# The first softmax of a packed attention: transposes on VectorE in 32x32 blocks, its product with v on tiles of 64 rows

## The chip, the cores and the metric

One core of a Trainium2 chip runs the kernel. The metric is the device time of one execution in microseconds. The kernel before took 729.4 us (median of three runs, 728.02 to 729.69). The engines are PE (matmuls; its weight loads are listed as PEld), DVE (VectorE), ACT (ScalarE), POOL (GpSimd) and SP, which issues most DMAs.

## The reference

The reference is an attention in two steps, followed by a feed-forward network. `q`, `k` and `v` have 8 batches, 8 heads, 576 tokens and 64 columns; `p` has 32 packed rows per head. Everything is float32.

```python
def sm_attn(qq, kk, vv):
    s = scale * np.matmul(qq, kk.transpose(0, 1, 3, 2))
    s = s - np.max(s, axis=-1, keepdims=True)
    a = np.exp(s)
    a = a / (np.sum(a, axis=-1, keepdims=True) + 1e-09)
    return np.matmul(a, vv)
p_packed = sm_attn(p, k, v)           # first softmax: 32 rows over 576 tokens
out = sm_attn(q, p_packed, p_packed)  # second softmax: 576 rows over 32
# x: the heads side by side, 4608 tokens x 512
h = x @ w_in                          # 512 x 2048
g = np.maximum(h, 0.0) + alpha * np.minimum(h, 0.0)
return g @ w_out                      # 2048 x 512
```

`w_in` and `w_out` arrive as 64-bit floats, seen as pairs of 32-bit words, and are converted on the chip.

## The kernel before, in words

**Dense part.** The outer loop runs over 16 halves of a batch (`k`, 288 tokens each) and 16 blocks of 128 hidden columns (`f`). One pair (k, f) is a *turn*. `first` makes the hidden block in PSUM from the second softmax and the product of the packed rows with `w_in` (six matmuls of 128x288 in two-part float32, L577 to L579), and applies the slope on ACT and DVE (L586, L587, L597, L598). `second` multiplies the block of two turns earlier (`AHEAD = 2`) with `w_out` (12 matmuls, L616 to L618). The first sweeps over batch 0 work in plain float32 (L574, L610). Results are evicted (L630 to L636) and stored by SP (L640).

**Attention of a batch** is a generator, `attention(b)`, that yields between its steps: loads; scores of the first softmax (`scores`, L320, through `in_turn`, L310); exponentials; transposes in two bursts; the product with v; the transpose of the packed rows (L449); the scores of the second softmax; then the second softmax itself (L462 to L500).

*First softmax (L354 to L402).* A group `r` (the even or the odd heads) has its four heads' 32 rows on the 128 partitions and all 576 tokens in its columns. ACT copies the scores out of PSUM (L368), DVE takes the maximum of each row (L392), ACT takes the exponential with its sum (L394), DVE makes the reciprocal of the sum (L397, L398). In batch 0 the maxima and exponentials read PSUM (L364, L384).

*Transposes (L409 to L424).* PE turns five blocks of 128 tokens per group against the identity (L419), ten a batch, and ACT evicts them as 384 and 256 columns (L422). The last block overlaps the fourth one by 64 tokens, where v is zeroed by POOL (L285, L296).

*Product with v (L428 to L447).* For each group, each of the five blocks and each of the four pairs of heads a matmul of 128 rows x 32 columns with 64 columns of v (L436), 40 a batch. Four of them lie side by side in the columns of PE's array. ACT scales the result with the reciprocal (L443).

**Loads.** `load` (L166) issues on SP in program order. `load_x` (L258) loads q and k, four tiles of 128 rows per batch; `load_v` (L277) loads v in eight DMAs per batch with runs of 512 bytes (in batch 0: four DMAs with runs of 2048 bytes). `w_in_load` (L218) loads `w_in` in eight pieces of 1 MB, one DMA of 128 rows each.

**Order.** Batches 0 and 1 (`b < EARLY`) are woven into the start and the first turns by hand, in the string given to `go` (L682) and in `pieces` (L699). From batch 2 on, step n of batch b is placed at turn `32 * (b - 1) + 3 + n`, two turns later for n > 7 (L702); a batch has 32 turns. A planner orders the instructions of each engine; `tc.issue_after` fixes what must stand behind what. `in_turn` puts a matmul behind the last dense one; from turn `STRICT = 48` on the dense matmuls keep the written order. In `go`, weight conversions stand behind the last ACT and DVE instructions of the attention's steps so far (`tail`, set by `anchor`, L332).

Of the kernel before, what the change touches and what calls it, by code (L numbers as in the profile page):

```python
# [27 lines left out]
def pack_attention_ffn_kernel(  # L28
# [21 lines left out]
    KT = (S + P - 1) // P  # L50
# [9 lines left out]
    VT = 4  # L60

    const = ctx.enter_context(tc.tile_pool(name="const", bufs=1))
    xin = ctx.enter_context(tc.tile_pool(name="xin", bufs=4))
    vin = ctx.enter_context(tc.tile_pool(name="vin", bufs=4))
# [153 lines left out]
    def w_in_load(n):  # L218
        j, h = n // 2, n % 2
        m = (4, 5, 6, 4, 4, 5, 6, 7)[n]  # L220
        if j == 0:
            src = w_in[:, h * 256 : (h + 1) * 256]
        else:
            src = w_in[2 * h * P : 2 * (h + 1) * P, j * 512 : (j + 1) * 512]
# [33 lines left out]
    def load_x(src, b, pool=None, tags=None, second=None):  # L258

        xs = []
        for pr in range(NP):
            if pool is None:
                x = xin.tile([P, S], F32, name="xraw", tag="xraw")
            else:
                if pr % 2 == 0:
                    two = pool.tile([P, 2, S], F32, name="xtwo", tag=tags[pr // 2])
                x = two[:, pr % 2]  # L270
            load(x, src[b, pr])
            if second is not None and pr == 0:
                load(*second)
            xs.append(x)
        return xs

    def load_v(b, tags=None):  # L277
        vs = []
        for pr in range(NP):
            if tags is None:  # L280
                raw = vin.tile([P, KT, P], F32, name="vraw", tag="vraw")
            else:
                if pr % 2 == 0:
                    two = const.tile([P, 2, KT, P], F32, name="vtwo", tag=tags[pr // 2])
                    nc.gpsimd.memset(two[: KT * P - S, :, VT, :], 0.0)  # L285
                    load(
                        two[:, :, :VT, :],
                        v[b, pr : pr + 2, : VT * P].rearrange("h (kp kt) d -> kp h kt d", kt=VT),
                    )
                    load(  # L290
                        two[KT * P - S :, :, VT, :],
                        v[b, pr : pr + 2, VT * P :].rearrange("h kp d -> kp h d"),
                    )
                vs.append(two[:, pr % 2])
                continue
            nc.gpsimd.memset(raw[: KT * P - S, KT - 1, :], 0.0)  # L296
            load(
                raw[:, : KT - 1, :],
                v[b, pr, : (KT - 1) * P].rearrange("(kt kp) d -> kp kt d", kp=P),
            )  # L300
            load(raw[KT * P - S :, KT - 1, :], v[b, pr, (KT - 1) * P :])
            vs.append(raw)
        return vs
# [6 lines left out]
    def in_turn(b, out, lhs, rhs):  # L310

        with ExitStack() as held:
            if b >= EARLY:
                held.enter_context(tc.issue_after(last_pe[0].ins))
            mm = nc.tensor.matmul(out, lhs, rhs, start=True, stop=True)  # L315
        last_mm[:] = [mm]
        if b >= EARLY:
            last_pe[:] = [mm]
# [12 lines left out]

    def anchor(b, a=None, d=None):  # L332
# [7 lines left out]
    def attention(b):  # L340
        praw = sm.tile([P, NP * N], F32, name="praw", tag="praw", bufs=2)
        packed = praw, pT[b].rearrange("p t n -> p (t n)")
        if b == 0:
            ks = load_x(kT, b, const, ("wo0", "wo1"), packed)
        else:
            load(*packed)
            ks = load_x(kT, b)
        yield
        if b < EARLY:
            vs = load_v(b, ("wo2", "wo3") if b == 0 else None)  # L350
            yield
            qs = load_x(qT, b, *((at, ("a", "a")) if b == 0 else ()))
            yield
        a = d = None  # L354
        in_psum = b < 1
        src, mx = {}, {}
        s_t = [wk.tile([P, S], F32, name="s_t", tag="w") for _ in range(2)]
        for hf in range(2):
            for r, ps in enumerate(scores(b, praw, ks, hf)):
                to = s_t[r][:, hf * HS : hf * HS + HS]  # L360
                if in_psum:
                    src[r, hf] = ps
                    mx[r, hf] = sm.tile([P, 1], F32, name="mx", tag="mx")
                    d = nc.vector.tensor_reduce(out=mx[r, hf], in_=ps, axis=AX.X, op=ALU.max)  # L364
                elif hf == 0 and b == 0:
                    d = nc.vector.tensor_copy(out=to, in_=ps)
                else:
                    a = nc.scalar.copy(out=to, in_=ps)  # L368
# [4 lines left out]
        dens = []  # L373
        for r in range(2):
            nmx = sm.tile([P, 1], F32, name="nmx", tag="nmx")
            den = sm.tile([P, 1], F32, name="den", tag="den")
            if in_psum:
                d = nc.vector.tensor_scalar(
                    out=nmx, in0=mx[r, 0], scalar1=mx[r, 1], scalar2=-SCALE, op0=ALU.max, op1=ALU.mult
                )  # L380
                anchor(b, None, d)
                dh = [sm.tile([P, 1], F32, name="dh", tag="dh") for _ in range(2)]
                for hf in range(2):
                    a = nc.scalar.activation(  # L384
                        out=s_t[r][:, hf * HS : hf * HS + HS], in_=src[r, hf], func=AF.Exp,
                        bias=nmx, scale=SCALE, accum_out=dh[hf],
                    )
                nc.vector.tensor_scalar(
                    out=den, in0=dh[0], scalar1=dh[1], scalar2=EPS, op0=ALU.add, op1=ALU.add
                )  # L390
            else:
                nc.vector.tensor_reduce(out=nmx, in_=s_t[r], axis=AX.X, op=ALU.max, negate=True)  # L392
                nc.vector.tensor_scalar(out=nmx, in0=nmx, scalar1=SCALE, scalar2=None, op0=ALU.mult)
                a = nc.scalar.activation(  # L394
                    out=s_t[r], in_=s_t[r], func=AF.Exp, bias=nmx, scale=SCALE, accum_out=den
                )
                nc.vector.tensor_scalar(out=den, in0=den, scalar1=EPS, scalar2=None, op0=ALU.add)  # L397
            d = nc.vector.reciprocal(out=den, in_=den)  # L398
            dens.append(den)
            anchor(b, a, None if in_psum else d)  # L400
# [3 lines left out]
        if b == 0:  # L404
            aT = [at.tile([P, KT, P], F32, name="aT", tag="a") for _ in range(2)]
        else:
            both = vin.tile([P, KT, 2, P], F32, name="aT", tag="aT", bufs=1)
            aT = [both[:, :, r] for r in range(2)]
        for r in range(2):  # L409
            for t0 in range(0, KT, 3):  # L410
                n = min(3, KT - t0)
                ps = bank()
                for i in range(n):
                    if b == 0 and t0 + i < VT:
# [362 lines left out]
```

## Time and profile before

| | |
|---|---|
| median of three runs | 729.4 us |
| profiled execution | 729.56 us |
| its span on the core | 727.7 us |
| PE busy | 709.6 us |
| DVE, ACT, POOL busy | 427.1, 362.6, 61.1 us |
| read from and written to memory | 70.79 and 13.63 MB |

The profile is of one execution on the chip. Busy time says how long an engine had something in work; matmuls are pipelined, so a busy PE need not be at its peak. The chain of waits is followed back from the last instruction to what released each step. In the rows further down, a line such as L419 is a line of the kernel before; `x5` is a count of instructions, and a float32 matmul has two records where it is made of two passes.

### The profile page before, as it was taken

To read this page: it belongs to the slowest core of one execution; us is meant where nothing else is said; L and a number is where in the kernel's file an instruction comes from. 1 tells how busy PE (TensorE), PEld (TensorE's weight loads), DVE (VectorE), ACT (ScalarE), POOL (GpSimd) and SP (SyncE) were. 2 spreads that over 40 slices of the span, in tenths; PEclk is the share of its full clock that TensorE was granted. 3 is DMA by queue.
4 is the path that set the end of the run, shared out by engine and by line. 5 is a ranking of instruction groups with operands and counts; after the bars stand their busy time and mean duration, and the time that the engine had idled before them with its cause. 6 is when DMAs were issued, how large, how long until landed. Compare 5 with 4: busy or idle time off the path is not lost.

```text
span 727.7 us, 15632 instructions
## 1 busy us (share of the span) xinstructions
PE 709.6 (98%) x6346; PEld 652.7 (90%) x6346; DVE 427.1 (59%) x859; ACT 362.6 (50%) x813; POOL 61.1 (8%) x80
## 2 busy tenths in 40 slices
PE   5799999999999999999999999999999999999998
PEld 3566898898998999999998999989999999999998
DVE  3898988858545474544645465454754538454443
ACT  3686688944435354453544534344444535443332
POOL 1001200002100040000300022000300004000000
PEclk9899999999999999999999999999999999999999
DMA  9996554234136223234034241261331501210001
GB/s 293 387 341 207 205 197 152 69 98 157 56 97 214 68 99 117 80 138 132 34 117 149 70 141 33 107 211 56 112 114 39 179 2 34 87 35 1 33 2 34
DMA packets 51386, 85.44 MB, mean 117 GB/s; under 512 B 4465, under 2 KB 31089, under 8 KB 51313
## 3 DMA queue, kind: packets, MB, share of 16 engines
q1 hardware_dynamic: 51024, 84.14, 34.3%
q8 instruction: 50, 0.82, 0.5%
q10 hardware_dynamic: 288, 0.30, 0.1%
q14 instruction: 24, 0.19, 0.1%
HBM read 70.79 MB, written 13.63 MB: 116 GB/s over the span
## 4 chain that ended last, share of the span: by engine, by line
PE 88%; DVE 5%; ACT 4%; DMA 1%; issue 1%; SPq 1%; ACTq 0%; DVEq 0%
PE acc L616 18%; PE acc L618 17%; PE acc L617 17%; PE ps_h L577 8%; PE ps_h L579 8%; PE ps_h L578 8%; PE ps_m L315 3%; PE ps_j L315 3%; PE ps_m L436 1%; DMA vtwo<-in_v 1%; PE ps_h L574 1%; PE ps_m L419 1%; ACT rest L161 1%; SPq L171 1%; ACT wo L208 1%
## 5 line engine op out<-in xcount | busy, mean ns | idle before, releaser
L616 PE MATMUL acc<-gh,wo 128*128 128x288 f32 x992 | 292.6, 301 | 0.9 <-DVE ot L630 0.7
L617 PE MATMUL acc<-gh,wo 128*128 128x288 f32 x992 | 287.3, 295 | 0.0
L618 PE MATMUL acc<-gl,wo 128*128 128x288 f32 x992 | 266.1, 296 | 0.0
L587 DVE SCALAR_TENSOR_TENSOR neg<-neg,nal,ps_h 128x288 f32<-128x288 f32 x248 | 126.7, 512 | 174.9 <-ACT neg L586 173.8
L616 PEld LDWEIGHTS acc<-gh,wo 128*128 128x128 f32 x992 | 186.1, 188 | 22.0 <-ACT pw L540 10.1
L586 ACT ACTIVATE neg<-ps_h 128x288 f32<-128x288 f32 x256 | 105.1, 411 | 190.1 <-PE ps_h L579 180.3
L617 PEld LDWEIGHTS acc<-gh,wo 128*128 128x128 f32 x992 | 186.3, 188 | 1.2 <-issue 0.8
L618 PEld LDWEIGHTS acc<-gl,wo 128*128 128x128 f32 x992 | 177.3, 188 | 0.1
L598 DVE TENSOR_TENSOR gl<-neg,gh 128x288 fp32r<-128x288 f32 x248 | 120.0, 487 | 68.2 <-ACT gh L597 65.0
L597 ACT CAST gh<-neg 128x288 fp32r<-128x288 f32 x248 | 106.9, 432 | 105.7 <-DVE neg L587 102.3
L579 PE MATMUL ps_h<-a_h,pw 128*128 128x288 f32 x480 | 141.9, 296 | 0.0
L578 PE MATMUL ps_h<-a_l,pw 128*128 128x288 f32 x480 | 141.9, 296 | 0.0
L577 PE MATMUL ps_h<-a_h,pw 128*128 128x288 f32 x480 | 141.6, 295 | 0.0
L577 PEld LDWEIGHTS ps_h<-a_h,pw 128*128 128x128 f32 x480 | 90.2, 188 | 0.1
L579 PEld LDWEIGHTS ps_h<-a_h,pw 128*128 128x128 f32 x480 | 90.1, 188 | 0.0
L578 PEld LDWEIGHTS ps_h<-a_l,pw 128*128 128x128 f32 x480 | 90.0, 188 | 0.0
L296 POOL MEMSET vraw<- 64x128 f32 x28 | 4.5, 198 | 346.9 <-PE ps_m L436 346.9
L473 POOL TENSOR_TENSOR t<-t,m 128x576 f32<-128x576 f32 x14 | 17.1, 1219 | 141.1 <-DVE m L471 141.1
L541 DVE SCALAR_TENSOR_TENSOR pw<-ps_j,pw 128x512 fp32r<-128x512 f32 x24 | 15.5, 686 | 13.8 <-ACT pw L540 13.8
L541 DVE SCALAR_TENSOR_TENSOR pw<-ps_m,pw 128x512 fp32r<-128x512 f32 x36 | 23.1, 681 | 0.2 <-ACT pw L540 0.2
L499 POOL TENSOR_TENSOR a_l<-s,a_h 128x576 fp32r<-128x576 f32 x14 | 20.2, 1442 | 29.6 <-ACT a_h L498 29.6
L315 PE MATMUL ps_m<-w,p 64*32 64x512 f32 (+1 forms) x352 | 22.2, 566 | 0.2 <-DVE w L135 0.2
(112 smaller groups left out, 538.5 us busy)
## 6 DMA issues: line engine op xcount, KB each, us to landing
w<-w_whole SPq DMA_DIRECT2D x48, 512.0 KB, 5.4
outT<-ot SPq DMA_DIRECT2D x62, 144.0 KB, 1.8
wraw<-in_w_in SPq DMA_DIRECT2D x8, 1024.0 KB, 10.3
wraw<-in_w_out SPq DMA_DIRECT2D x8, 1024.0 KB, 6.9
xraw<-in_kT SPq DMA_DIRECT2D x28, 288.0 KB, 4.0
xraw<-in_qT SPq DMA_DIRECT2D x28, 288.0 KB, 3.9
vraw<-in_v SPq DMA_DIRECT2D x28, 256.0 KB, 3.5
w_whole<-w SPq DMA_DIRECT2D x6, 512.0 KB, 7.2
```

The costliest lines, as they stand in the source:

```text
L315: mm = nc.tensor.matmul(out, lhs, rhs, start=True, stop=True)
L541: nc.vector.scalar_tensor_tensor(out=lo, in0=ps, scalar=times, in1=fv(hi), op0=ALU.mult, op1=ALU.subtract)
L577: nc.tensor.matmul(x, w[:, 0, i], a_h[:, i], start=(i == 0), stop=False)
L578: nc.tensor.matmul(x, w[:, 0, i], a_l[:, i], start=False, stop=False)
L579: mm = nc.tensor.matmul(x, w[:, 1, i], a_h[:, i], start=False, stop=(i == 1))
L586: nc.scalar.activation(out=neg, in_=x, func=AF.Relu, scale=-1.0),
L587: nc.vector.scalar_tensor_tensor(out=g, in0=neg, scalar=nal[:, f : f + 1], in1=x, op0=ALU.mult, op1=ALU.add),
L597: late[:] = [nc.scalar.copy(out=gh, in_=g)]
L598: nc.vector.tensor_tensor(out=gl, in0=g, in1=fv(gh), op=ALU.subtract)
L616: nc.tensor.matmul(ps, wo_t[f][:, 0, os_], gh, start=begin, stop=False)
L617: nc.tensor.matmul(ps, wo_t[f][:, 1, os_], gh, start=False, stop=False)
L618: mm = nc.tensor.matmul(ps, wo_t[f][:, 0, os_], gl, start=False, stop=end)
```

## The change

- The scores of the first softmax are laid out anew (`first_scores`): tile `s` (two of the four pairs of heads), within it group `r` in its columns, and on the partitions pair `e`, half `hf` of the tokens and 32 rows. Each softmax row so lies on two partition ranges, with 288 tokens in each.
- The maximum and the sum of a row are put together across the two ranges: the maximum on DVE (`highest`: four scalings of 32 rows and one combination per tile), the sum by 16 copies of 32x1 on POOL, one addition and one reciprocal on DVE.
- Scores are written with a stride of 32 elements, so that one DVE transpose per tile, in blocks of 32x32, gives the operand of the product. The transposes on PE and their evictions on ACT are gone.
- The product contracts 64 rows (32 places of both halves of the tokens): 72 matmuls of 64 rows x 32 columns a batch, eight side by side, through `in_turn`. Batch 0 does tile 0 before tile 1.
- v is loaded in two DMAs a batch with 4608 contiguous bytes per partition; q in four DMAs of 64 partitions; `w_in` in four DMAs of 64 partitions for each of the first two pieces and two for each other one. k comes in two DMAs a batch from batch 1 on.
- Steps n = 6 and 7 (the product and the transpose of the packed rows) come one turn later, and `STRICT` is 52.

```diff
-    VT = 4
+    KT = HS // 32
+    QUARTERS = [(2 * a + hf, 2 * s + r) for a in range(2) for hf in range(2) for s in range(2) for r in range(2)]
 def w_in_load(n):
-        src = src.rearrange("(a p) d -> p a d", p=P)
-        raws["i", n] = const.tile([P, src.shape[1], src.shape[2]], U64, name=f"wraw{m}", tag=f"wo{m}")
-        load(raws["i", n], src)
+        for a in range(2):
+            to = raw[a * 64 : a * 64 + 64]
+            for s in range(2) if j == 0 else (h,):
+                rows = slice((2 * s + a) * P, (2 * s + a + 1) * P)
+                if j == 0:
+                    src, here = w_in[rows, h * 256 : h * 256 + 256], to[:, 2 * s : 2 * s + 2]
+                else:
+                    src, here = w_in[rows, j * 512 : j * 512 + 512], to
+                load(here, src.rearrange("(r d) c -> d r c", r=2))
+    def load_q(b):
...
+            for a in range(2):
+                load(
+                    two[a * 64 : a * 64 + 64],
+                    qT[b, 2 * s + a].rearrange("(r d) t -> d r t", r=2),
+                )
+    def load_v(b):
...
+            load(raw, v[b, 2 * s : 2 * s + 2].rearrange("a (p kt) d -> (a p) kt d", kt=KT))
+    def first_scores(b, st, xs, s):
...
+        for e in range(2):
+            pr = 2 * s + e
+            for hf in range(2):
+                to = slice(e * 64 + hf * 32, e * 64 + hf * 32 + 32)
+                for r in range(2):
+                    rs = slice(r * 64, r * 64 + 64)
+                    in_turn(
+                        b, banks[r][to, :HS], st[rs, pr * N : pr * N + N],
+                        xs[pr][rs, hf * HS : hf * HS + HS],
+                    )
+        def highest(cols):
+            for q in range(4):
+                o = (q ^ 1) * 32
+                nc.vector.tensor_scalar(
+                    out=sw[q * 32 : q * 32 + 32, cols], in0=mx[o : o + 32, cols],
+                    scalar1=-SCALE, scalar2=None, op0=ALU.mult,
+                )
+            return nc.vector.scalar_tensor_tensor(
+                out=nmx[:, cols], in0=mx[:, cols], scalar=-SCALE, in1=sw[:, cols],
+                op0=ALU.mult, op1=ALU.min,
+            )
+                    a = nc.scalar.copy(out=turned(s_t[s][:, r]), in_=by_run(ps))
...
-                    nc.tensor.transpose(out=ps[:, i * P : i * P + P], in_=in_, identity=ident)
-                a = nc.scalar.copy(out=to, in_=in_)
+        for s in range(2):
+            d = nc.vector.transpose(out=aT[:, s], in_=s_t[s])
+            anchor(b, None, d)
+            if s:
+                for frm, to in QUARTERS:
+                    nc.gpsimd.tensor_copy(
+                        out=dn[to * 32 : to * 32 + 32, frm : frm + 1],
+                        in_=den[frm * 32 : frm * 32 + 32, to : to + 1],
+                    )
...
+        for s_ in (range(1), range(1, 2)) if b == 0 else (range(2),):
             for kt in range(KT):
-                for pr in range(NP):
-                    cs = slice(pr * N, pr * N + N)
-                            ps[cs, rs], aT[r][:, kt, cs], vs[pr][:, kt, rs],
+                for s in s_:
+                    for r in range(2):
+                        to = slice((2 * s + r) * 32, (2 * s + r) * 32 + 32)
+                        for e in range(2):
+                            rs = slice(e * 64, e * 64 + 64)
+                            in_turn(
+                                b, banks[e][to, :64], aT[rs, s, r, kt * 32 : kt * 32 + 32],
+                                vs[s][rs, kt, r * 64 : r * 64 + 64],
+                                start=(kt == 0), stop=(kt == KT - 1),
+                            )
...
-        add(attention(b), [T + 3 + n + 2 * (n > 7) for n in range(17)], (T + 4, T + 13))
+        add(attention(b), [T + 3 + n + (n > 5) + (n > 7) for n in range(17)], (T + 4, T + 13))
-    AHEAD, STRICT = 2, 48
+    AHEAD, STRICT = 2, 52
```

## Rows read from the trace of the kernel before

**Rows 1.** The page: busy time and count of each engine; shares of the chain.
```profile
PE 709.6 (98%) x6346; PEld 652.7 (90%) x6346; DVE 427.1 (59%) x859; ACT 362.6 (50%) x813; POOL 61.1 (8%) x80
...
PE 88%; DVE 5%; ACT 4%; DMA 1%; issue 1%; SPq 1%; ACTq 0%; DVEq 0%
```
**Rows 2.** Windows: stretch, length, busy us per engine, granted clock, DMA share, GB/s.
```profile
0.00:12.00 12.00, 5.37 (x33) 2.08 (x33) 2.77 (x8) 2.75 (x7) 2.25 (x14) 1.00 0.83 261
12.00:24.00 12.00, 9.81 (x148) 6.56 (x148) 6.44 (x13) 5.79 (x16) 0.00 (x0) 0.61 1.04 374
24.00:36.00 12.00, 8.55 (x43) 6.03 (x50) 11.90 (x20) 9.96 (x11) 0.00 (x0) 0.96 1.06 386
48.00:60.00 12.00, 11.31 (x79) 8.08 (x82) 11.96 (x20) 10.41 (x21) 0.00 (x0) 1.00 1.03 406
227.00:313.00 86.00, 86.00 (x800) 80.91 (x798) 45.96 (x99) 39.24 (x96) 8.44 (x10) 1.00 0.33 106
```
**Rows 3.** Timeline of PE (start, us, instruction) around a burst of transposes.
```profile
237.87 0.29 PE L577 MATMUL ps_h<-a_h,pw 128*128 128x288 f32 x1
238.00 0.71 PE L419 MATMUL ps_m<-ident,s_t 128*128 128x128 f32 x5
...
238.67 0.30 PE L579 MATMUL ps_h<-a_h,pw 128*128 128x288 f32 x1
```
**Rows 4.** Timeline of PE around the product with v of one batch.
```profile
244.79 0.29 PE L618 MATMUL acc<-gl,wo 128*128 128x288 f32 x1
245.01 1.32 PE L436 MATMUL ps_m<-vraw,aT 128*32 128x64 f32 x80
246.26 0.40 PE L616 MATMUL acc<-gh,wo 128*128 128x288 f32 x1
246.50 0.29 PE L617 MATMUL acc<-gh,wo 128*128 128x288 f32 x1
```
**Rows 5.** Timeline of PE, second scores, window from 252.51 to 252.572.
```profile
252.52 0.47 PE L315 MATMUL ps_j<-xraw,p 64*32 64x288 f32 x8
```
**Rows 6.** Chain of waits (start, us, what) at the second scores, their second half.
```profile
253.24 0.48 PE ps_m L315 x16
```
**Rows 7.** Groups of DVE by line: out<-in, shapes, count, busy us, mean ns, idle.
```profile
L497 DVE STREAM_TRANSPOSE s<-t 128x576 f32<-128x576 f32 x14 | 10.8, 770 | 0.2 <-POOL t L481 0.2
...
L392 DVE TENSOR_REDUCE nmx<-s_t 128x1 f32<-128x576 f32 x14 | 10.4, 746 | 0.0
...
L393 DVE TENSOR_SCALAR nmx<-nmx 128x1 f32<-128x1 f32 x14 | 2.1, 147 | 0.0
```
**Rows 8.** Groups of ACT by line, the copies of the first scores.
```profile
L368 ACT COPY s_t<-ps_m 128x288 f32<-128x288 f32 x16 | 5.9, 416 | 1.9 <-PE ps_m L315 1.9
```
**Rows 9.** Groups of POOL by line, two small operations.
```profile
L296 POOL MEMSET vraw<- 64x128 f32 x28 | 4.5, 198 | 346.9 <-PE ps_m L436 346.9
...
L658 POOL TENSOR_SCALAR nal<-al 128x16 f32<-128x16 f32 x1 | 0.4, 443 | 8.9 <-DMA al<-in_alpha 8.9
```
**Rows 10.** Chain of waits in the start, from v's load to the second scores.
```profile
5.70 9.16 DMA vtwo<-in_v
...
14.90 1.30 PE ps_m L436 x36
...
16.59 1.36 PE ps_m L436 x40
...
18.35 0.49 PE ps_m L449
...
19.18 1.17 PE acc L315 x9
```
**Rows 11.** Timeline of SP's queue: the first loads of w_in, v and q.
```profile
3.08 0.43 SPq L171 DMA_DIRECT2D wraw<-in_w_in  x1
...
4.10 3.49 SPq L171 DMA_DIRECT2D vtwo<-in_v  x4
7.63 4.16 SPq L171 DMA_DIRECT2D xtwo<-in_qT  x4
```

More of the change, by code (lines that the diff above doesn't have):

```diff
@@ L254, in keep_busy, with load_k @@
                 last_mm[:] = [nc.tensor.matmul(spare[:, :P], ident, ident, start=True, stop=True)]
-    def load_x(src, b, pool=None, tags=None, second=None):
+    def load_k(b, second):
         xs = []
-        for pr in range(NP):
-            if pool is None:
-                x = xin.tile([P, S], F32, name="xraw", tag="xraw")
-            else:
[L268 to L274, printed above, removed]
-        return xs
@@ L277, in load_v @@
-    def load_v(b, tags=None):
+        for s in range(2):
+            if b == 0:
+                two = const.tile([P, 2, S], F32, name="xtwo", tag=f"wo{s}")
+                for e in range(2):
+                    load(two[:, e], kT[b, 2 * s + e])
+                    if s + e == 0:
+                        load(*second)
+            else:
+                two = xin.tile([P, 2, S], F32, name="xraw", tag="xraw")
+                load(two, kT[b, 2 * s : 2 * s + 2].rearrange("e p t -> p e t"))
+            xs += [two[:, e] for e in range(2)]
@@ new lines, in load_k @@
+        return xs
+    def load_q(b):
+        xs = []
+        for s in range(2):
+            if b == 0:
+                two = at.tile([P, 2, S], F32, name="xtwo", tag="a")
+            else:
+                two = xin.tile([P, 2, S], F32, name="xraw", tag="xraw")
+            for a in range(2):
[3 more added lines that the diff above has]
+                )
+            xs += [two[:, r] for r in range(2)]
+        return xs
@@ L278, in load_v @@
+    def load_v(b):
         vs = []
-        for pr in range(NP):
-            if tags is None:
+        for s in range(2):
+            if b == 0:
+                raw = const.tile([P, KT, P], F32, name="vtwo", tag=f"wo{2 + s}")
+            else:
                 raw = vin.tile([P, KT, P], F32, name="vraw", tag="vraw")
[L282 to L301, printed above, removed]
@@ L372, in attention @@
             vs = load_v(b)
[L373 to L379, printed above, removed]
-                )
[L381 to L400, printed above, removed]
+        for s in range(2):
+            cols = slice(2 * s, 2 * s + 2)
+            if not in_psum:
+                nc.vector.tensor_reduce(out=mx[:, cols], in_=s_t[s], axis=AX.X, op=ALU.max)
+                d = highest(cols)
+            for r in range(2):
+                col = slice(2 * s + r, 2 * s + r + 1)
+                if in_psum:
+                    to, in_ = turned(s_t[s][:, r]), by_run(src[s, r])
+                else:
+                    to = in_ = s_t[s][:, r]
+                a = nc.scalar.activation(
+                    out=to, in_=in_, func=AF.Exp, bias=nmx[:, col], scale=SCALE, accum_out=den[:, col]
+                )
+            anchor(b, a, d)
             if b == 0:
@@ L446, in attention @@
+        halves = dn.rearrange("p (e f) -> p f e", f=2)
+        nc.vector.scalar_tensor_tensor(
+            out=rden, in0=halves[:, 0], scalar=EPS, in1=halves[:, 1], op0=ALU.add, op1=ALU.add
+        )
+        d = nc.vector.reciprocal(out=rden, in_=rden)
+        anchor(b, None, d)
+        for e in range(2):
+            a = nc.scalar.activation(
+                out=c[:, e * 64 : e * 64 + 64], in_=banks[e][:, :64], func=AF.Copy,
+                scale=rden[:, e : e + 1],
+            )
         anchor(b, a)
```

100 lines of the change are left out of this document (42 added, 58 removed).

## The prediction, made before the changed kernel was run

> **What bounds the kernel now.** I read the page first: PE is busy 98% of the span and the chain that ended last runs 88% over PE [rows 1]. An average can hide stages, so next the table by stage [rows 2]: between 227 and 313 us, one batch's period of 86 us, PE is busy for all 86.00 us, DVE for 45.96, ACT for 39.24, POOL for 8.44 and the DMA engines for a third, at a granted clock of 1.00. There, whatever leaves PE shortens the period by as much, and work added to DVE, ACT or POOL costs nothing as long as it comes in time. The start is different. [...] So the change has two prices: one in the PE-bound periods, one in a start bound by loads and DVE.
>
> **PE in a PE-bound period.** Removed: ten transposes a batch, in two bursts of five. Matmuls of the dense work follow each other every 0.131 us. From the L577 ahead of a burst to the L579 behind it is 238.67 - 237.87 = 0.80 us, where two steps would take 0.26: a burst costs 0.54 us, two cost 1.08 [rows 3].
>
> The product with v: now 40 matmuls, in float32 two records each, 80 records. It takes, from L618 at 244.79 to L617 at 246.50, 1.71 us less the 0.26 of two steps: 1.45 us. The product itself fills 245.01 to 246.26, 1.25 us [rows 4]. Four 32-column tiles run side by side, so these are 20 rounds of 0.0625 us; the other 0.20 is getting in and out. After: 2 (s) x 2 (r) x 2 (e) x 9 (kt) = 72 matmuls, 144 records, eight tiles of 64 rows x 32 columns side by side: 18 rounds. Does PE keep eight such tiles going? The scores are of this shape: eight records have begun by 252.572, where the first began at 252.52 [rows 5], so one every 0.007 us, and a round of eight can be issued in 0.052 us, less than the 0.0625 of a round. [...] So 18 x 0.0625 = 1.13 us, with the same 0.20: a gain of 0.12.
>
> [...]
>
> Sum: -1.08 - 0.12 = -1.20 us a batch. Batches 2 to 7 lie in the PE-bound part: 6 x 1.20 = **-7.2 us**.
>
> **What is hidden in those periods.** DVE loses a 128x1 negation-scaling and an add per group and two reciprocals, keeps its two maxima (746 ns each), and gains two transposes of 128x576 (770 ns in the row of the same shape), eight quarter-sized scalings, two combinations and the joint denominator, twelve tiny operations at about 0.15 us [rows 7]. Before: 2 x 0.75 + 6 x 0.15 = 2.4 us a batch; after: 1.5 + 1.54 + 12 x 0.15 = 4.8; so +2.4 us into 40 us that DVE has idle. ACT loses the four evictions of the transposes, gains two shorter exponentials, and writes its four score copies (416 ns each, [rows 8]) with a stride of 32 elements, for which the trace has no row: between 416 ns and a doubled 832, that is at most +1.7 us into 46 us of idle time. POOL loses four memsets and gains 16 copies of 32x1; its rows are 198 ns for a memset and 443 for a small scaling [rows 9], so 3 to 7 us, beside two turns of PE's dense work. If this cover is gone, the product waits, since it now holds a fixed place on PE, one turn later than before; what waits behind it is all dense work. Two turns lie between the last DVE transpose and the product, so I take zero. SP issues fewer loads (v is 2 instead of 8 per batch) and the loads of q have most of a batch to land.
>
> **Batch 1** has its first softmax in the DVE-bound start. PE gains the same 1.2 us there, DVE gets 2.4 us more in stretches where it was idle for 0.1 us of 12 [rows 2]. If PE alone counts: -1.2; if DVE alone: +2.4. I take the middle, **+0.7**, and keep both ends.
>
> **Batch 0 and its loads.** The chain of the start waits for v until 14.86, then for the product in two parts (1.30 and 1.36 us at the lower clock), the scaling, the transpose of c and its eviction; the second scores begin at 19.18 [rows 10]. After the change only the part of the product that needs the second half of v stays behind the load: 72 records on four tiles, 18 of the 20 rounds that took 2.66 us: 2.4 us, so c's transpose begins some 0.4 us earlier. DVE's transposes end before v lands. The first w_in conversion on DVE now stands behind these transposes, some 3 us later; it has until 20 us, and DVE is busy only 6.44 of 12 us there [rows 2]. POOL's 16 copies have from the last exponential to the end of the product, some 4 us: enough at 198 ns, not at 443 (+2.6).
>
> But ahead of v in SP's queue stands w_in's first piece, behind it q [rows 11], and both are now loads onto 64 rows: the piece of 1.05 MB as four loads, q's 1.18 MB as four. The trace has no large load onto 64 rows. At the saturated 374 to 386 GB/s they take 2.8 and 3.1 us as now. The slowest stretch of the start moved 261 GB/s: 4.0 and 4.5. Now q lands at about 18.0 (v's 14.86 and 1.18 MB at 374 GB/s); it would land 0 to 2.6 us later, v 0 to 1.2. I take the upper end, as half the rows is a change of shape for the worse: the second scores at 20.6 in place of 19.18, +1.4. The second w_in piece, one of the next in the queue, is late by as much again as the first; for what its conversion can't absorb I put 0.5. Together **+1.9 us** on all that follows, as DVE has no room to make it up.
>
> **The sum** against the profiled execution (729.56 us, span 727.7; the median of three runs, 729.4, is 0.16 lower): -7.2 + 0.7 + 1.9 = -4.6, so **725.0 us**; with the bounds of batches 0 and 1 and half of the product's, 722 to 728.
>
> **Rivals.**
> - *Loads onto 64 rows run at half the rate.* Then at 187 to 193 GB/s the w_in piece takes 5.5 us for 2.75 and q 6.1 for 3.05: q 5.8 us later, at 23.8, the second scores +4.6, and the same 0.5 for the second w_in piece: +5.1 on the start in place of +1.9, 728.2 us. For it: the saturated queue in 12 to 36 us [rows 2]. Against: the later pieces land well ahead of need, so it is paid once. [...]
> - *PE issues one record per 0.0156 us, whatever the tiles.* Place: the product. 144 x 0.0156 = 2.25 us in place of 1.13; it decides from the point where a round of eight takes over 0.0625 us to issue. 6 x 1.12 = +6.7 us: 731.7, **slower** than before. For it: that is the product's pace today [rows 4]. Against: the eight that began within 0.052 us [rows 5].
> - *The start hides its additions.* Loads as fast as now and DVE's extra in its gaps: -7.2 - 1.2 - 0.4 = -8.8: 720.8 us. Against it: the full DVE and DMA stretches [rows 2].
>
> **How the numbers follow.** The forecast gets 0.42, the half-rate loads 0.25, the hidden start 0.15, the issue-bound product 0.10; 0.08 is left for what I haven't seen (a late transpose that makes the product wait in every batch would cost up to a turn of 18 dense steps, 2.4 us, each, 14 us). A measurement of this kernel can tell 0.2%, 1.5 us: faster is below 727.9, slower above 730.9. Faster: 0.42 of the forecast, 0.12 of the half-rate case, the hidden start, 0.03 of the rest: 0.72. Slower: the issue-bound product and half of the rest: 0.14. Same: 0.14. The range that leaves out the slower cases and the tip of the hidden start: 720.5 to 729.5.
>
> **What would show it.** No PE row of the transposes but c's; the product's 144 records in 1.0 to 1.2 us between L618 and L616; a period 1.2 us shorter than now, with PE still busy throughout. In the start: the landing of v and q, the time of the second scores (19.18 now) and of the first dense matmuls, DVE's share from 24 to 60 us. The prediction is wrong if the product takes over 2 us, if PE waits ahead of it for DVE's transposes, or if the start moves by more than 5 us.

## The result, and the profile after

The changed kernel is slower: 739.06 us (median of 4 runs, 737.85 to 741.42) where the kernel before took 729.43 in the same runs, a ratio of 1.014 (95% interval 1.0111 to 1.0169). Forecast were 725.0 us, and a range of 720.5 to 729.5. The profiled execution took 739.63 us, with a span of 737.8.

The page after, busy time and chain, against [rows 1]:

```profile
PE 706.7 (96%) x6778; PEld 646.1 (88%) x6778; DVE 445.7 (60%) x923; ACT 362.8 (49%) x809; POOL 83.0 (11%) x178
...
PE 86%; DMA 8%; ACT 2%; DVE 2%; issue 1%; SPq 1%; ACTq 0%
```

PE is busy 2.9 us less than before, as it should be, yet the span is 10.1 us longer. What is new stands in the chain: DMA, 1% before, is 8%. The same windows as in [rows 2]:

```profile
0.00:12.00 12.00, 4.73 (x32) 0.82 (x32) 3.45 (x14) 2.85 (x6) 2.16 (x15) 1.00 0.84 208
12.00:24.00 12.00, 6.36 (x163) 4.57 (x171) 5.75 (x10) 3.28 (x8) 2.10 (x9) 1.00 1.04 268
24.00:36.00 12.00, 7.35 (x64) 4.80 (x48) 7.42 (x14) 5.84 (x8) 0.00 (x0) 1.00 1.05 253
48.00:60.00 12.00, 11.82 (x69) 7.80 (x66) 9.03 (x22) 10.24 (x21) 2.51 (x8) 1.00 1.03 351
227.00:313.00 86.00, 86.00 (x858) 81.02 (x858) 49.28 (x109) 38.93 (x94) 10.84 (x22) 1.00 0.33 106
```

The last two columns are to be read together. The DMA engines are as full as before (1.04 and 1.05), but from 24 to 36 us they move 253 GB/s in place of 386: busy, and slow. DVE, 11.90 us busy there before, has fallen to 7.42: this stretch is no longer bound by DVE but by loads. The PE-bound period in the last row looks as before.

The chain of waits from 0 to 92 us (start, us, what) shows how long that lasts:

```profile
5.12 8.95 DMA wraw<-in_w_in
14.15 0.39 SPq L171
14.59 15.13 DMA wraw<-in_w_in
29.74 14.19 DMA wraw<-in_w_in
43.99 12.23 DMA wraw<-in_w_out
56.28 9.18 DMA wraw<-in_w_in
```

One raw piece of weights after another holds the chain, from 5 to 65 us, and SP's next issue stands right behind a landing (14.15 behind 5.12 + 8.95 = 14.07): a slow load holds back the issue of later ones too. In both traces none of the loads issued up to 60 us goes out before the one eight earlier has landed (the issue at 14.15 is such a case). And PE's waits over the whole span (us in all, times, longest):

```profile
PE acc L640 <- DVE g L617: 6.2, 1, 6.2
PE ps_m L318 <- DMA vtwo<-in_v: 5.5, 1, 5.5
...
PE acc L646 <- issue: 1.9, 2, 1.1
```

The largest is not the wait for v but one from 33.8 to 40.0 us, for DVE's g. In DVE's order g stands behind conversions of weights that landed late: ACT, which begins a conversion, stood 2.66 us for a raw piece until 33.73, and DVE 2.88 us for ACT. The product with v in a PE-bound period, against [rows 4]:

```profile
253.40 0.29 PE L609 MATMUL ps_h<-a_h,pw 128*128 128x288 f32 x1
253.62 1.66 PE L318 MATMUL ps_m<-vraw,aT 64*32 64x64 f32 x144
255.21 0.40 PE L646 MATMUL acc<-gh,wo 128*128 128x288 f32 x1
255.45 0.29 PE L647 MATMUL acc<-gh,wo 128*128 128x288 f32 x1
```

From L609 to L647 2.05 us less two steps of 0.13: a detour of 1.79 us, where the old one was 1.45.

What DVE, ACT and POOL got (groups by line, mean ns behind the busy us):

```profile
L438 DVE STREAM_TRANSPOSE aT<-s_t 128x576 f32<-128x576 f32 x16 | 12.4, 775 | 5.1 <-ACT s_t L426 5.1
L391 DVE TENSOR_SCALAR sw<-mx 32x2 f32<-32x2 f32 x64 | 10.3, 161 | 1.1
L408 ACT COPY s_t<-ps_m 128x288 f32<-128x288 f32 x16 | 10.3, 721 | 1.7 <-PE ps_m L318 1.7
L442 POOL COPY dn<-den 32x1 f32<-32x1 f32 x128 | 27.0, 211 | 355.1 <-ACT s_t L426 350.3
```

Where the 10.1 us of span came from, by three landmarks of the timeline (start of the second scores, of the first and of the hundredth acc<-gh matmul):

| | second scores | first acc<-gh | 100th | end |
|---|---|---|---|---|
| before | 19.18 | 64.72 | 98.93 | 727.7 |
| after | 22.15 | 77.44 | 111.63 | 737.8 |
| difference | +2.97 | +12.72 | +12.70 | +10.1 |

So the start loses 12.7 us, 9.75 of them behind the second scores, and the other 630 us win back some 2.5.

### The profile page after: what moved, and what is told of

The parts are those of the page before. It is cut to its first block, busy times and chain, and to the rows that moved or that the text cites. A ratio compares the mean times of both kernels' runs of the same rounds, so it can differ in the third digit from the quotient of the medians.

```text
span 737.8 us, 16561 instructions
## 1 busy us (share of the span) xinstructions
PE 706.7 (96%) x6778; PEld 646.1 (88%) x6778; DVE 445.7 (60%) x923; ACT 362.8 (49%) x809; POOL 83.0 (11%) x178
## 4 chain that ended last, share of the span: by engine, by line
PE 86%; DMA 8%; ACT 2%; DVE 2%; issue 1%; SPq 1%; ACTq 0%
PE acc L646 18%; PE acc L647 17%; PE acc L648 17%; PE ps_h L609 8%; PE ps_h L607 8%; PE ps_h L608 8%; DMA wraw<-in_w_in 6%; PE ps_m L318 4%; PE ps_j L318 3%; DMA wraw<-in_w_out 2%; PE ps_h L604 1%; SPq L171 1%; ACT wo L208 1%; ACT rest L161 1%; DVE wo L209 0%
## 5 line engine op out<-in xcount | busy, mean ns | idle before, releaser
L647 PE MATMUL acc<-gh,wo 128*128 128x288 f32 x992 | 287.1, 295 | 0.0
L648 PE MATMUL acc<-gl,wo 128*128 128x288 f32 x992 | 262.8, 294 | 0.0
L646 PEld LDWEIGHTS acc<-gh,wo 128*128 128x128 f32 x992 | 185.9, 188 | 22.3 <-ACT pw L570 10.1
L647 PEld LDWEIGHTS acc<-gh,wo 128*128 128x128 f32 x992 | 186.2, 188 | 2.1 <-issue 1.8
L609 PE MATMUL ps_h<-a_h,pw 128*128 128x288 f32 x480 | 141.7, 295 | 0.0
L609 PEld LDWEIGHTS ps_h<-a_h,pw 128*128 128x128 f32 x480 | 90.1, 188 | 0.0
L442 POOL COPY dn<-den 32x1 f32<-32x1 f32 x128 | 27.0, 211 | 355.1 <-ACT s_t L426 350.3
L640 PE MATMUL acc<-g,wo_whole 128*128 128x288 f32 x64 | 19.2, 450 | 6.2 <-DVE g L617 6.2
L318 PE MATMUL ps_m<-w,p 64*32 64x512 f32 (+1 forms) x352 | 24.0, 566 | 0.0
L640 PEld LDWEIGHTS acc<-g,wo_whole 128*128 128x128 f32 x64 | 13.3, 212 | 12.3 <-DVE g L617 6.7
```

Source lines behind the costliest of these rows:

```text
L318: mm = nc.tensor.matmul(out, lhs, rhs, start=start, stop=stop)
L609: mm = nc.tensor.matmul(x, w[:, 1, i], a_h[:, i], start=False, stop=(i == 1))
L640: nc.tensor.matmul(ps, wo_t[f][:, os_], g, start=begin, stop=end)
L646: nc.tensor.matmul(ps, wo_t[f][:, 0, os_], gh, start=begin, stop=False)
L647: nc.tensor.matmul(ps, wo_t[f][:, 1, os_], gh, start=False, stop=False)
L648: mm = nc.tensor.matmul(ps, wo_t[f][:, 0, os_], gl, start=False, stop=end)
```

## The experiments

All ratios are to the kernel before, timed on the same chip. Unless said otherwise an interval is 95%.

**1. Is it the shape of the loads?** Theory L: the loads onto 64 rows cost the start its time. Theory D: DVE's (and ACT's) added work does. Three kernels lay the heads of w_in, of q, or of both out in the new order ahead of the launch, so that each is loaded onto 128 rows as before; all else is as changed.

```
-        for a in range(2):
-            to = raw[a * 64 : a * 64 + 64]
...
-                load(here, src.rearrange("(r d) c -> d r c", r=2))
...
+            src = w_in[2 * h * P : 2 * (h + 1) * P, j * 512 : (j + 1) * 512]
+        src = src.rearrange("(a p) d -> p a d", p=P)
...
+        load(raws["i", n], src)
...
-            for a in range(2):
-                load(
-                    two[a * 64 : a * 64 + 64],
-                    qT[b, 2 * s + a].rearrange("(r d) t -> d r t", r=2),
-                )
+            for r in range(2):
+                load(two[:, r], qT[b, 2 * s + r])
```

Both: 

> The changed kernel with w_in and q laid out by the host in the order of heads that it needs, so that each piece of w_in is one load of 128 rows again and q is four loads of 128 rows; all else is as in the changed kernel (739.1 us). Theory L (loads onto 64 rows run at half the rate and the start waits for them): the start is back near that of the kernel before (second scores near 19 us), the periods stay 0.85 us shorter: 722 to 727 us. Rival D (DVE's and POOL's additional operations in the start are what is late): no gain, 736 to 740 us.

w_in alone: 

> As the run before, but w_in alone in loads of 128 rows; q stays on 64 rows. Theory L: w_in is 8.4 of the 10.8 MB that the start loads onto 64 rows, so most comes back, less q's 3 us ahead of the second scores: 725 to 731 us. Rival D: 736 to 740 us.

q alone: 

> q alone in loads of 128 rows; w_in stays on 64 rows. Theory L: little comes back, as w_in's pieces hold the queue: 734 to 738 us. Rival D: 736 to 740 us.

Measured: both 728.74 us (0.9984, 0.9973 to 0.9995); w_in alone 732.66 (1.0043, 1.0026 to 1.0061); q alone 733.46 (1.0058, 1.0037 to 1.0079). So the 64-row loads cost 739.06 - 728.74 = 10.3 us, 6.4 of it come back with w_in alone and 5.6 with q alone (together more than 10.3, so the two overlap): theory L, and D's 736 to 740 is out each time. But L's own figures are all missed, for both together (722 to 727), for w_in alone (725 to 731) and for q alone (734 to 738, q counts for more); some 4 us are left to find.

**2. The rows, or the number of loads?** The kernel before, with each w_in piece cut in two halves of 64 rows; in two halves of the columns on 128 rows; and in three loads, of rows 32 to 95, 0 to 31 and 96 to 127.

```
-        load(raws["i", n], src)
+        for e in range(2):                                   # 64 rows
+            load(raws["i", n][e * 64 : e * 64 + 64], src[e * 64 : e * 64 + 64])
...
+        wide = src.shape[2] // 2                             # columns
+        for e in range(2):
+            load(raws["i", n][:, :, e * wide : e * wide + wide], src[:, :, e * wide : e * wide + wide])
...
+        for rows in (slice(32, 96), slice(0, 32), slice(96, 128)):
+            load(raws["i", n][rows], src[rows])
```

Rows: 

> The kernel before (729.4 us), with each piece of w_in loaded in two halves of 64 rows (0 to 63, 64 to 127), all else unchanged. Theory L: a piece takes 5.3 us of the queue in place of 2.6, and the start is late by most of what the change cost: 735 to 741 us. Rival N (more DMAs in a queue that holds eight at a time): the same. Rival D: 729 to 731 us.

Columns: 

> The kernel before, with each piece of w_in loaded in two halves of its columns, 128 rows each: as many DMAs as with the halves of 64 rows, as many bytes each. Theory L: 729 to 731 us. Rival N: as slow as the halves of 64 rows, 735 to 741 us.

Middle rows: 

> The kernel before, with each piece of w_in loaded as rows 32 to 95, rows 0 to 31 and rows 96 to 127. [...] Rival R (the rate goes by the number of rows alone): 2.6 us for the middle and 2.6 for each outer quarter, 7.9 us a piece: 743 to 755 us.

Measured: halves of rows 734.63 (1.0071, 1.0054 to 1.0088), just under theory L's 735 to 741; of columns 729.7 (1.0001, 0.9991 to 1.001); middle rows 731.92 (1.0039, 1.0029 to 1.005). The view of the transfers, 0 to 50 us, gives what was moved; the five lines are from before, after, halves of rows, of columns, and middle rows (other loads of the start are in them too):

```profile
DMA packets 9773, 16.74 MB, mean 335 GB/s; under 512 B 811, under 2 KB 4651, under 8 KB 9770
```
```profile
DMA packets 5376, 12.32 MB, mean 246 GB/s; under 512 B 633, under 2 KB 1401, under 8 KB 5373
```
```profile
DMA packets 8048, 12.84 MB, mean 257 GB/s; under 512 B 741, under 2 KB 3949, under 8 KB 8045
```
```profile
DMA packets 11156, 16.27 MB, mean 325 GB/s; under 512 B 846, under 2 KB 6734, under 8 KB 11152
```
```profile
DMA packets 8605, 14.31 MB, mean 286 GB/s; under 512 B 832, under 2 KB 4160, under 8 KB 8603
```

Twice as many loads cost nothing (325 GB/s); half the rows take the rate to 257, in the kernel before too. The price of the shape by itself is larger than these means say. In the kernel with halves of rows, the two halves of one w_in piece land at 27.0 and 29.4 us and a w_out piece on 128 rows right behind them, at 32.0 (windows as in [rows 2]):

```profile
25.00:28.00 3.00, 2.97 (x18) 2.78 (x18) 2.22 (x6) 2.44 (x3) 0.00 (x0) 0.70 1.08 218
29.50:32.00 2.50, 2.11 (x5) 1.63 (x6) 2.13 (x5) 2.50 (x3) 0.00 (x0) 0.64 1.03 382
```

At the same full share a load onto 64 rows moves 218 GB/s where one onto 128 rows moves 382: a little over half.

The third kernel has three loads a piece, one of them of 64 rows also, and at 731.92 us lies between 729.7 and 734.63 (286 GB/s between 325 and 257), not in the range of rival R (743 to 755), by which the number of rows alone would count. That speaks for which rows a load spans, not for how many; what makes the difference no run shows.

**3. The product, in two bursts.** In 1.445 us its 144 records begin unevenly: 11, 15, 7 and 6 in the first four tenths of a microsecond, then 8 to 12 in each up to the last. Theory Q: the first records were ready ahead and go at 0.007 us each, the rest at the pace at which PE issues, some 0.0107; then each of two bursts would have a quick beginning.

```
             for kt in range(KT):
+                if b >= EARLY and kt == 5:
+                    yield
...
```

> The kernel with all loads on 128 rows, the product with v of batches 2 to 7 in two bursts (80 and 64 records) a turn apart. Theory Q (PE begins a burst with about 34 records ready, one per 0.007 us, and then gets one per 0.0107 us): the records take 0.75 + 0.58 = 1.33 us in place of 1.445, the second entry and exit cost 0.34: periods 0.2 us longer, the time +1 to +2 us against the kernel in one burst. Rival T (eight tiles of 64 rows get in each other's way at any time, 0.0100 us a record from the first): 1.445 us in all, periods 0.34 longer, +2 us; the counts of records by tenths of a microsecond tell them apart.

Measured, on top of the 128-row loads: 730.47 us (1.0003, 0.9989 to 1.0017), so no faster than in one burst (728.74). PE's timeline of one batch:

```profile
245.18 1.04 PE L310 MATMUL ps_m<-vraw,aT 64*32 64x64 f32 x80
...
248.71 0.86 PE L310 MATMUL ps_m<-vraw,aT 64*32 64x64 f32 x64
```

Both bursts begin 11, 15, 7, 6 per tenth again, so each of the two has the quick beginning, as theory Q says. But it is worth nothing: from the first to the last start the two take 0.82 + 0.64 = 1.46 us, where Q had 1.33 and one burst takes 1.445. The second time of getting in and out comes on top (detours of 1.17 and 0.99 us for one of 1.79), and a period grows from 85.03 to 85.37, by the 0.34 of rival T and not by Q's 0.2. Q's pace of 0.007 for 34 records is also not quite what the starts show: the first 32 begin within 0.24 us, in rounds of eight that are 0.056 us apart from the second on, and the other 112 take the 1.18 us from 0.27 on, 0.0106 each. Why the pace falls there stays open.

**4. What the other 4 us are.** On the kernel with all loads on 128 rows: batch 1 without its eight scalings and two transposes on DVE; with plain copies of scores; with both. And the change without part of it: batches 0 and 1, or batch 1 alone, with the old first softmax.

```
+            if b == 1:                                # without DVE's work: one scaling for four
+                return nc.vector.tensor_scalar(
+                    out=nmx[:, cols], in0=mx[:, cols], scalar1=-SCALE, scalar2=None, op0=ALU.mult
+                )
             for q in range(4):
...
+            if b != 1:
+                d = nc.vector.transpose(out=aT[:, s], in_=s_t[s])
...
+                                s_t[s][rs, r, kt * 32 : kt * 32 + 32] if b == 1
...
+                    if b == 1:                        # plain copies
+                        a = nc.scalar.copy(out=s_t[s][:, r], in_=ps)
...
+        if b in OLD:                          # (0, 1) or (1,)
+            c = yield from as_before(b, praw, ks, vs)
```

Less DVE: 

> The kernel with all loads on 128 rows (728.7 us), with two pieces of batch 1 left out on VectorE: the eight scalings of 32 rows (8 x 0.160 = 1.3 us; each 64 rows then take the maximum of their own half of the tokens) and the two block transposes (2 x 0.772 = 1.5 us; the product reads the exps untransposed, so batch 1's values are other ones). Theory D (the start is bound by VectorE, and what batch 1 adds there comes on top): 725.5 to 727 us, first dense matmul at 64.5 to 66 (67.28 with them). Theory A (ScalarE's strided copies of scores and the wait behind them cost the start's time, VectorE's own work does not): 728 to 729.5. Theory C (what is lost between 30 and 100 us has to do with neither): 728 to 729.5.

Plain copies: 

> The kernel with all loads on 128 rows (728.7 us), with batch 1's four copies of scores written in order instead of at a stride of 32 elements (the columns that the transposes and the product then take are other ones; the work is the same). Theory A (the strided writes, 0.69 us each for 0.395, and VectorE's 2.0 us of waiting for them, lose the start's time): 726 to 727.5 us, first dense matmul at 65 to 66. Theory D (VectorE's added work): no more than the 4 x 0.29 = 1.2 us that VectorE waits less, 727.5 to 728.7. Theory C: 728 to 729.5.

Batches 0 and 1 as before: 

> The change for batches 2 to 7 only: batches 0 and 1 take their first softmax, transposes and product with v as in the kernel before, with their k, v and packed queries laid out in the new order of heads, and all loads on 128 rows. Theories D and A (the work of batches 0 and 1 in the start is what ate the rest of the gain): the start is that of before (first dense matmul at 64.7) and six periods gain 0.85 us each, 729.5 - 5.1 = 724.4 us (723 to 726). Theory C (the loss does not hang on batches 0 and 1): 727.5 to 729.

Batch 1 as before: 

> As the one with batches 0 and 1 as before, but with batch 0 in the new way again (its second scores came 1.2 us earlier with all loads on 128 rows). If batch 1's added work alone ate the gain (theory D or A) and the earlier second scores count: 723 to 724.5 us. If VectorE is the bound from the loads on, whatever batch 0 saves: as with both as before, 724 to 726. If batch 0's new form loses time too: 1 to 3 us above the one with both as before.

Less DVE and plain copies: 

> All loads on 128 rows (728.7 us), batch 1 without the eight scalings and the two block transposes on VectorE and with its four copies of scores written in order (its values are other ones). Without the first pair alone it took 728.3, with plain copies alone 727.0, with batch 1 wholly in the old way 724.8. Theory B (VectorE and ScalarE share the bound there, and either alone hides the other): 724.5 to 726 us. Theory S (the two are separate and small): 728.7 - 0.4 - 1.7 = 726.6, 726 to 727.2. Theory K (the loss is the clock's, granted at half in the stretch of the first a_f and wo_whole matmuls, and neither edit touches it): 726.5 to 728.5.

Measured: less DVE 728.33 (0.9979, 0.9968 to 0.9989); plain copies 726.98 (0.9962, 0.9947 to 0.9977); both 727.66 (0.997, 0.996 to 0.998); batches 0 and 1 as before 725.56 (0.9944, 0.993 to 0.9958); batch 1 as before 724.76 (0.9935, 0.992 to 0.9949), both in the range that D and A gave. So the loss lies in batch 1's new form, 728.74 - 724.76 = 4.0 us, as theories D and A had it, and leaving batch 1 out beats both kernels. Which piece of it costs the time these removals don't say. Less DVE alone is not told apart from 728.74, which is A's and C's figure and not D's; plain copies are at A's figure (726 to 727.5); but both together, at 727.66, are no better than plain copies alone, and B (724.5 to 726) and S (726 to 727.2) miss it. Only K (726.5 to 728.5), which puts the loss on PE's clock, is met there; it is tested in 6.

DVE's waits from 30 to 66 us in the run without both pieces give a reason why less work did not help:

```profile
DVE mx L417 <- ACT s_t L405: 1.8, 1, 1.8
DVE wo L209 <- ACT wo L208: 1.2, 1, 1.2
DVE rden L468 <- POOL dn L442: 0.8, 1, 0.8
```

With its own work gone, DVE stands 0.8 us at the joint sum (`rden`), for the last of POOL's sixteen copies, with conversions queued behind. The run less DVE alone has the same wait, 0.8 us. It isn't in the kernel that has the work: there the copies are done first. The copies themselves are also longer with the work gone, 7.1 us for the sixteen against 5.3.

**5. The pieces added one by one, and POOL's copies taken away.** To the version with batch 1 as before: eight scalings and two transposes on DVE that nothing reads; or strided copies of scores. From the version without both pieces: the sixteen copies.

```
+            if b == 1:
...
+                nc.vector.transpose(out=spare_t, in_=s_t[r])        # and 4 tensor_scalar of 32 rows, twice
...
-            if s:
+            if s and b != 1:                                        # POOL's copies
                 for frm, to in QUARTERS:
```

Without POOL's copies: 

> As the run without batch 1's scalings and transposes and with plain copies (727.7 us), and without batch 1's sixteen copies of sums on GpSimd, for which VectorE's reciprocal waited 0.8 us there with the rest of VectorE's work behind it (the rows are divided by other sums; batch 1's values are other ones). Theory W (what is left of batch 1's cost is such a wait in VectorE's order): 726 to 727.2, first dense matmul 0.8 us earlier after the first wo_whole matmul (35.46 us there). Rival (the product's 144 records and the exps in four pieces are what is left): 727.3 to 728.

DVE work added: 

> The version with batch 1's first softmax as before (724.8 us) plus, in batch 1, eight scalings of 32 rows and two 128x576 block transposes on VectorE that nothing reads (8 x 0.160 + 2 x 0.772 = 2.8 us). Theory D (VectorE bounds the start, so what batch 1 adds there counts in full): 726.8 to 728, first dense matmul 2 to 3 us later. If VectorE's work hides behind something else, as the run without it suggested: 724.5 to 725.7.

Strides added: 

> The version with batch 1's first softmax as before (724.8 us), with its four copies of scores written at a stride of 32 elements (4 x 0.29 = 1.2 us more of ScalarE; the tokens stand in another order than v's, so batch 1's values are other ones). Theory A (VectorE's maxima wait for them, in the bound stretch): 725.7 to 726.8. If ScalarE has slack there: 724.3 to 725.5.

Measured: DVE work added 727.93 (0.9974, 0.9963 to 0.9985), about 3 us over the 724.76 that it began from (0.992 to 0.9949, so well apart); strides 725.67 (0.9946, 0.9934 to 0.9957), 0.9 us, which these intervals don't tell from none; without POOL's copies 725.43 (0.9942, 0.9929 to 0.9955), 2.2 us under the 727.66 that it began from, and below theory W's 726 to 727.2. So the 2.8 us of DVE work count in full where they are added (theory D's 726.8 to 728), and where they are gone POOL's copies count in their place. PE's first acc<-gh matmul, first without the added work and then with it (the tile's view: durations, then first and last start):

```profile
L760 PE MATMUL acc<-gh,wo x992: 288/294/515, 63.6 to 718.6; 128*128 128x288 f32 x199
```
```profile
L771 PE MATMUL acc<-gh,wo x992: 288/294/512, 68.0 to 722.2; 128*128 128x288 f32 x199
```

These two executions lie 4.4 us apart there, somewhat more than the medians. And in DVE's waits of the run without the copies the row of rden is gone:

```profile
DVE mx L417 <- ACT s_t L405: 1.8, 1, 1.8
DVE wo L209 <- ACT wo L208: 1.2, 1, 1.2
DVE w L124 <- ACT w L119: 0.5, 1, 0.5
```

The profile shows 0.8 us of waiting where the runs show some 2 us of time; what the rest is stays open.

**6. Two more.** Theory K: the loss is PE's clock. In the profile with 128-row loads it is granted at 0.50 in one stretch of the first a_f matmuls and at 0.61 in a later one (windows of 4 us). The run with batch 1 as before has its low stretch earlier (0.66 from 20 to 24 us) and 1.00 from 24 us on:

```profile
28.00:32.00 4.00, 2.13 (x5) 1.12 (x4) 4.00 (x6) 3.21 (x4) 0.00 (x0) 0.50 1.02 404
32.00:36.00 4.00, 4.00 (x14) 2.78 (x13) 3.86 (x6) 1.40 (x2) 0.00 (x0) 0.81 1.04 406
...
68.00:72.00 4.00, 4.00 (x29) 2.54 (x28) 2.95 (x5) 1.37 (x3) 0.00 (x0) 0.61 0.01 4
```

The test gives PE 11 more of the kernel's matmuls of the identity ahead of a_f (`BUSY = {"x": 17, "y": 3}` for 6).

> All loads on 128 rows (728.7 us), and 11 more of the matmuls of the identity that the kernel already issues behind the second scores (9 of them end at 22.7 us and PE then waits 2.9 us for a_f): PE is busy until a_f is there. Theory K (the half clock at 27 to 34 us and again at 68 to 71 us follows from that wait and is what most runs lose): 726 to 727.5, granted clock 1.00 from 24 to 36 us. If the clock costs nothing there or does not follow from the wait: 728 to 730, up to 1.5 us later where the added matmuls end behind a_f.

Measured: 729.92 us (1.0, 0.9987 to 1.0013), not faster than 728.74. The clock falls all the same, to 0.57 from 32 to 36 us; only the later fall is gone (1.00 from 68 to 72 us). So these matmuls don't mend it, and as they didn't keep the clock up in the first stretch, they don't rule K out there. How much of one execution the clock takes is not settled. Single executions lie 3 to 5 us apart (726.74 to 730.13 with 128-row loads), and of all profiles only two have the later fall, the one above and that of the run with plain copies: each is of its kernel's slowest execution. The medians hang on it little: of the ten executions with 128-row loads the six at a mean granted clock of 0.998 have a median of 728.74, the four at 0.992 to 0.995 one of 728.93.

The other moves the scalings from batch 2 on to POOL (`(nc.gpsimd if b >= EARLY else nc.vector).tensor_scalar`), with batch 1 as before.

> The version with batch 1's first softmax as before (724.8 us), and from batch 2 on the eight scalings of 32 rows on GpSimd instead of VectorE. Theory V (in batch 2's turn VectorE is 11.1 us busy of 12 and PE waits 1.1 us for its neg; later turns have slack): the scalings' 1.3 us go, 0.5 to 1.2 us faster, 723.6 to 724.3. Rival (GpSimd takes longer for each and ScalarE's exps, behind them in ScalarE's order, hold back gh): 0 to 2 us slower, 724.8 to 727.

Measured: 725.33 us (0.9933, 0.9916 to 0.9951), not told apart from 724.76, so theory V's gain (723.6 to 724.3) did not come. The wait in batch 2's turn (98 to 172 us) did shrink, from the first line to the second:

```profile
PE ps_h L721 <- DVE neg L731: 1.1, 2, 0.6
```
```profile
PE ps_h L721 <- DVE neg L731: 0.5, 1, 0.5
```

## Why the prediction was wrong

- **Batch 0 and its loads: the step that failed.** Forecast were +1.9 us for this term; the loads alone measured 10.3, and by the prediction's own sign of being wrong (a start that moves by more than 5 us) the start moved by 12.7. Two things in the term were wrong. First, the rate: the price of 64 rows was bounded from below by "as now" and from above by the slowest stretch of the start, 261 GB/s, a stretch of 128-row loads at a DMA share of 0.83. No row showed the shape, so no row bounded it; measured were 218 GB/s. Second, and larger, the bytes: the rate was applied to w_in's first piece and to q, 2.2 MB, and the later pieces got 0.5 us in all.
- **The half-rate rival had the rate nearly right and too small a price.** It took 187 to 193 GB/s, half of the 374 to 386 of [rows 2]; that half was an assumption, as no row showed the shape, and the runs showed 218 against 382. Its w_in piece (5.5 us) and q (6.1) set the second scores back by 4.6. Measured were 2.97 against the kernel before, and 4.16 against the kernel with 128-row loads, whose second scores begin at 17.99: batch 0's new form with its other loads brings them 1.2 us earlier, where 0.4 was forecast. What the rival left out is behind them. "The later pieces land well ahead of need, so it is paid once" was wrong: the chain shows five raw pieces end to end until 65 us, and 9.75 of the 12.72 us come after the second scores. The saturated share in [rows 2] runs on to 60 us; the price of a rate is the bytes of all of it, not those up to the first consumer. By 65 us four pieces of w_in and two batches of q, 6.6 MB, land onto 64 rows; at 218 in place of some 390 GB/s (between the 374 and 406 of [rows 2]) that is an estimated 13 us of the queue.
- **Batch 1: outside both ends.** The middle of -1.2 and +2.4 was taken, as +0.7 (it is +0.6). The experiments give +4.0, about 3 of it DVE's added work, which [rows 7] had sized near enough (+2.4): where DVE is idle for 0.1 us of 12, only that end of the bound was left. What makes up the remaining 1 us is open; strided copies gave 0.9, not told from none. POOL's copies, weighed only for batch 0, are what is late next.
- **The transposes go: right.** The product: mis-sized. Their 1.08 us went. The product was to fill 18 x 0.0625 = 1.13 us from its first record to the dense matmul behind it; it fills 253.62 to 255.21, 1.59 us (1.25 in [rows 4]). That a round of eight keeps to the 0.0625 us of a round of four was the author's estimate: no run shows it, and here it takes 0.081 (8 x 0.0101) in the mean. The eight that had begun at once in [rows 5] were the quick beginning of a burst, which lasts for 32 records here; in the mean a record begins every 0.0101 us. So the detour grew by 0.34 in place of shrinking by 0.12: by these rows a gain of 0.74 us a period in place of 1.20. From product to product a period went from 85.87 (mean of four) to 85.02 (three of four), by 0.85. The issue-bound rival (0.0156 each, 2.25 us) was too pessimistic; whether it is issuing that sets the pace was not tested.
- **Hidden work in the PE-bound periods: right but for batch 2.** DVE's busy time from 227 to 313 us rose by 3.3 us (45.96 to 49.28; 2.4 forecast), ACT and POOL have room, and no later product waits for a transpose. But batch 2's turn, from 144 to 156 us, is not PE-bound: DVE is 11.1 us busy of 12 there with batch 1 as before, PE waits 1.1 us for neg, and between the 100th and 300th acc<-gh matmul 0.87 us are lost where 0.85 were to be won.
- **A cost nobody forecast:** PE's 1.9 us of "issue" between the dense matmuls, in two pieces; one of them, 0.8 us, falls into the one period that took 86.01 us. Ten of the fifteen profiles with the new product have 0.5 to 1.9 us of it behind 172 us, none of the four of the kernel before and its variants. Its cause wasn't tried.

In one sum of medians: +10.3 (64-row loads), +4.0 (batch 1) and -4.7 for the rest (724.76 - 729.43; -7.2 was forecast for batches 2 to 7) make the +9.6 that was measured. Each term is the step from one of these kernels to the next, so the sum comes out by construction and is no further evidence.

## What to carry to other kernels

When a change alters the shape of a load, price it over every byte that shares the queue until it empties, and where no row shows the shape, measure the load alone before trusting a bound from other shapes. A cost on an engine with no idle time is to be counted in full, as here with DVE's 2.8 us (some 3 us measured); taking it away may only bring up the next wait in the same queue, so test a suspect by adding it to the fast version as well as by removing it from the slow one. A rate read from the first few records of a burst is not the rate of the burst (0.007 us a record in the first eight, 0.0101 over all 144).

## What the runs showed of the hardware

- Loads onto rows 0 to 63 or 64 to 127 moved 218 GB/s with the DMA engines at a full share, loads onto 128 rows 382 in the same run; over the first 50 us, with all other loads, 246 to 257 GB/s against 325 to 335.
- 144 records of small matmuls on eight tiles of 64x32 began 0.0101 us apart in the mean: 32 in the first 0.24 us, the others 0.0106 apart. From the first start to the next dense matmul that is 0.0110 a record, against the 0.0156 of four tiles in [rows 4].
- ACT's copy of 128x288 from PSUM takes 707 to 721 ns (means of the two groups in the changed kernel) when it writes at a stride of 32 elements, 416 in order [rows 8]. The bound of a doubled 832 held.
- A 32x1 copy on POOL takes 211 ns in the mean, near the memset of [rows 9] and not the 443 of the small scaling: 191 from batch 2 on, but 334 in batch 1:

```profile
L434 POOL COPY dn<-den 32x1 f32<-32x1 f32 x16 | 5.3, 334 | 33.5 <-ACT s_t L418 32.9
```

That row is of the kernel with 128-row loads, 28 to 68 us: sixteen copies, 5.3 us in all. Less work on DVE did not shorten them (408 ns without its own work of batch 1, 441 with plain copies as well); what lengthens them there was not tested.
